# Lightning attention and a SiLU layer on one core: how the decay rates are spread, the gates of the first loads, the turn of set 5 and the form of one product are changed

## Chip, cores and metric

The kernel runs on one core of a Trainium2 chip. The metric is the device time of one execution in microseconds (us). The kernel before takes 201.95 us, the median of three runs (201.56 to 202.51).

## What is computed

The inputs are q, k, v of shape (4 batches, 8 heads, 768 positions, 64), one decay rate `lam` per head, and the weights `w_in` (512 x 2048) and `w_out` (2048 x 512), all float32.

1. Attention with decay, block by block of 64 positions (12 blocks). Inside a block, `out = ((q k^T) * Dmask) v`, with `Dmask[i,j] = lam^i` for `i >= j` and 0 elsewhere. From the blocks before, `out += (q * lam^(i+1)) state`. Then `state = lam^64 * state + (k * lam^(63-i))^T v`.
2. The heads are laid side by side: x has 3072 rows of 512 numbers.
3. `h = x w_in`, `g = h * sigmoid(h)` (SiLU), `out = g w_out`.

Nearly all arithmetic is in the two dense products of step 3.

## The kernel before

**Units, sets, groups.** A unit is 128 positions of one batch, (n, b) with n = 0..5 and b = 0..3. Units are numbered by their turn: units 0 to 7 are those of n = 0 and 1 (two of each batch in turn), units 8 to 23 are n = 2 to 5. A set is two units that are loaded together (twelve sets; sets 0 to 3 are the paired blocks n = 0, 1 of a batch, sets 4 to 11 two batches of one n). A group is the set of units whose x is multiplied by `w_in` together: groups 0 to 3 are sets 0 to 3 (256 rows), groups 4 to 7 have four units (512 rows).

**The path of a set.** SyncE's queue (SP) loads q, k, v as float32 into `raw` (512 KB each, `load_set`, L382, issued in L394 and L399). VectorE (DVE) and ScalarE (ACT) scale and cast them to bfloat16 (`kq`, `vd`). q, k are then turned (positions and features exchanged) into `kqT`: for sets below TURNED = 6 by TensorE (PE) through a bank of PSUM, matmuls `tr` of L535 (sets 0 to 3) and L722 (sets 4 and 5), and a copy by DVE or ACT; from set 6 on by a transposing DMA on SP's queue (L731). Scores (`st_ps`, L610, L766), states (`d_ps`, L557, L756) and outputs (`x_ps`, L636, L641, L788, L796) follow on PE, with masks and state sums on DVE between them. The result is copied to `xt`.

**The dense products.** Product 1 (`product1`, L917, matmuls L934, SiLU L946) takes `xt` and `w_in_bf`; half of group 6 and all of group 7 use `product1_spared` (L1052), a Strassen-like form with 7 products of blocks in place of 8. Product 2 has a plain form (`product2_plain`, L956, matmul L969: 16 matmuls of 512 columns for a unit, then one copy and one store) for the first PLAIN = 4 units, and a spared form (`product2`, L1120, matmuls L1182) for every four units after that: 7 products of 16 matmuls of 256 columns. The spared form needs 16 sums of g on DVE for each four units (L1142), and sums of `w_out` made once (`sums_of_w_out`, L1101).

**The rates.** `lam` (8 numbers) is loaded into all 128 partitions by one DMA on ACT's queue (L277). ACT takes the logarithm (L326, L328) and exponentials with a scale for each partition (L334 to L337); these multiply q, k's carry and v. ACT then loads the table for SiLU (L338). DVE first clears the six `xe` tiles (L287) and makes the scales `pose` (L321, L322).

**Weights.** POOL's queue (GpSimd) loads `w_in` in pieces i0, i1a, i1b, i2, i3 (L420) and `w_out` in o0 to o3 (L423), float32 in DRAM and bfloat16 in SBUF. A gate is a small copy (L374) on POOL, or a tiny DMA (L453) on SP, that waits for one load; what is behind it on its queue comes later. SEQUENCE (L246) gives the order: `i0@0.2` is i0 behind a gate on load 2 of set 0. Load 0 is k, 1 is q, 2 is v; for sets 0 to 3 q is issued first.

```
SEQUENCE = "s0 i0@0.2 s1 i1a@0.2 i1b i2 i3 o0 o1 s2@1.2 o2 o3 s3 s4"
```

**The order of the work** is made by a planner (class `Planner`, L38) when the program is built: each task has a key and a cost, the planner simulates engines, buffers and transfers, and emits each engine's instructions in the order of its simulated time. On the chip each engine runs its list in that order. The numbers in L35 to L47 (bytes and ns of a packet, when an engine begins, when a transfer starts and lands, until when PE is slow) are only estimates of the planner: they change the order, not the work. `filler` (L1264) puts matmuls of `ident` that nobody reads into PE's idle time at the start (between DENSE[0] and THIN).

Of the kernel before, what the change touches and what calls it, by code (L numbers as in the profile page):

```python
# [8 lines left out]
F32 = mybir.dt.float32  # L9
BF16 = mybir.dt.bfloat16  # L10
AF = mybir.ActivationFunctionType
AL = mybir.AluOpType
# [19 lines left out]

SMALL, WIDE, CAST, LARGE, HALF, TURN, PART = (256, 17.5, 20.0), (512, 25.0, 28.0), (256, 14.0, 31.0), (2048, 86.0, 86.0), (1024, 58.0, 58.0), (1024, 50.0, 50.0), (1024, 45.0, 45.0)  # L35


class Planner:  # L38
# [3 lines left out]
    OVERLAP = {"ACT": 0.1, "DVE": 0.09}  # L42
    BEGIN = {"PE": 0.8, "ACT": 7.7, "DVE": 4.5, "POOL": 4.7, "SP": 0.8}
    BIAS = {"DVE": 0.2}
    SLOW, SLOWER = 14.0, 1.8
    DENSE, THIN, REST = (9.6, 17.0), 24.0, 0.3
    FIRST, LAST, AHEAD = {"SP": 1.7, "ACT": 1.15, "POOL": 3.0}, 1.0, 0.75  # L47

    def __init__(self, pools):
        self.pools = {n: list(range(c)) for n, c in pools.items()}  # L50
# [12 lines left out]
    def order(self):  # L63
# [7 lines left out]
        free = dict(self.BEGIN)  # L71
# [56 lines left out]
        while len(out) < len(self.tasks) + fillers:  # L128
# [9 lines left out]
            for e in free:  # L138
# [2 lines left out]
                    heapq.heappush(ready[e], (key, i, t))  # L141
                if free[e] > now:
                    continue
                if e == "SP" and sum(j[2] for j in queues[e]) > self.AHEAD:
                    continue
                kept, took, short = [], None, set()
                while ready[e]:
# [53 lines left out]
                    if not u.left:  # L201
                        arm(u)
                if t.nbytes:
                    start = max(free[e] + self.FIRST[e], queues[e][-1][1] if queues[e] else 0.0)
                    queues[e].append([t, start, t.nbytes, t.kind])
                    after = transfer(now)
                else:
                    t.end = free[e] + self.LAT[e]
                    finish(t, e)
# [7 lines left out]
def kernel(  # L217
# [24 lines left out]
    PAIRED = 2  # L242
    SETS = [[(0, b), (1, b)] for b in range(B)] + [[(n, b), (n, b + 1)] for n in range(PAIRED, NB) for b in (0, 2)]
    GROUPS = SETS[:4] + [[(n, b) for b in range(B)] for n in range(PAIRED, NB)]
    FRESH, TURNED, ALONE, LEAD = 4, 6, 6, 4.5
    SEQUENCE = "s0 i0@0.2 s1 i1a@0.2 i1b i2 i3 o0 o1 s2@1.2 o2 o3 s3 s4"  # L246
    POOLS = dict(bank=8, ra=3, rb=6, kq=3, kqT=3, vd=3, st=3, xe=6, xf=3, y=2, yf=2,
                 xt2=2, xt4=2, g=18, s=12, m=3, osb=3, one=3, two=8, att=6, sp=2)
    BY_POOL, PLAIN = (), 4
    CASTING, SUMS_AFTER, HURRY, SUMS_ON, HOLD, ONTO = 12, 16, 0.0, 9.0, 1, 24  # L250
    EARLY, PACE = 1.0, 1.0
    OPEN, FILLED, SCALED = 4, True, ()
    QUERIES = (0, 1, 2, 3)
    SCORED, SOON, HALVED = (0, 1), 3, 0
    ON_ACT = ()
    LAZY, FINE, SAFE = 2.0, True, 0.3
    XE_2, XE_B, XE_P = {"ACT": 0.42, "DVE": 0.35}, 0.1, False
    MIXED, APART, KEPT = (0, 1), 1, "yf"
    EAGER, CALM, ON = 8.0, 1.0, 0.0

    ctx.enter_context(tc.manual_schedule())
    const = ctx.enter_context(tc.tile_pool(name="const", bufs=1))
# [6 lines left out]
    def tile_of(b, shape, dt, name):  # L269
# [3 lines left out]
        return b.tile  # L273


    lam_sb = const.tile([128, H], F32, name="lam_sb")
    nc.scalar.dma_start(  # L277
        out=lam_sb,
        in_=bass.AP(tensor=lam.tensor, offset=lam.offset, ap=[[0, 128]] + list(lam.ap)),
    )  # L280
    nc.scalar.preload_act_table_set("natural_log_exp_and_others")

    halves = [slice(0, 64), slice(64, 128)]
# [41 lines left out]
    log_lam = const.tile([128, NP], F32, name="log_lam")  # L325
    nc.scalar.activation(log_all, lam_sb, AF.Ln)  # L326
    for h, r in enumerate(halves):
        nc.scalar.activation(log_lam[r], lam_sb[r, h::2], AF.Ln)  # L328
    lam_v, lam_q = [const.tile([128, H], F32, name=f"lam_{x}") for x in "vq"]
    lam_v2, lam_q2 = [const.tile([128, H, 2], F32, name=f"lam_{x}2") for x in "vq"]  # L330
    lam_be = const.tile([128, NP], F32, name="lam_be")
    for i, t in ((1, lam_q2), (0, lam_v2)):
        for a in range(2):
            nc.scalar.activation(t[:, :, a], log_all, AF.Exp, scale=pose_2[:, i, a:a + 1])  # L334
    for i, t in enumerate((lam_v, lam_q)):
        nc.scalar.activation(t, log_all, AF.Exp, scale=pose[:, i:i + 1])
# [45 lines left out]
    def load_set(key, si):  # L382
        n, b = sets[si][0]
        nb = 2
        rs = [Buf("rb") if si >= CASTING and i == 0 else None if si >= CASTING and i == 1 else Buf("ra" if si in (0, 3) else "rb")
              for i in range(3)]
        ts = []
        x = [t[b, :, 0:2 * U, :].rearrange("h (p e) d -> p h (e d)", e=2) if n < PAIRED else
             t[b:b + 2, :, n * U:n * U + U, :].rearrange("b h s d -> s (b h) d") for t in (k, q, v)]

        def go(e, i):
            if n < PAIRED:
                tile_of(rs[i], [128, H, 2, 64], F32, "raw")
                nc.sync.dma_start(out=rs[i].tile.rearrange("p h e d -> p h (e d)"), in_=x[i])  # L394
            elif si >= CASTING and i < 2:
                tl = tile_of(rs[0], [128, 2, 2, NP, 2, 64], BF16, "kq")
                nc.gpsimd.dma_start(out=tl[:, i].rearrange("p b m h d -> p (b m h) d"), in_=x[i])
            else:
                nc.sync.dma_start(out=tile_of(rs[i], [128, 2 * H, 64], F32, "raw"), in_=x[i])  # L399

        for i in (1, 0, 2) if si in QUERIES else range(3):
            if si >= CASTING and i < 2:
                t = pool_task(add((key, i), {"POOL": 0.8}, lambda e, i=i: go(e, i), bufs=[rs[0]], nbytes=0.524, kind=CAST,
                                  prior=pool_last[-1:] + raw[si - 1][1][2], late=2.0))
                ts.append([t])
# [10 lines left out]
    def load_w(key, what, j, part):  # L416
        def go(e):
            if what == "i":
                cs = {"": slice(512 * j, 512 * j + 512), "a": slice(512 * j, 512 * j + 256), "b": slice(512 * j + 256, 512 * j + 512)}[part]
                nc.gpsimd.dma_start(out=w_in_bf[:, :, cs], in_=w_in_r[:, :, cs])  # L420
            else:
                ks = slice(4 * j, 4 * j + 4)
                nc.gpsimd.dma_start(out=w_out_bf[:, ks, :], in_=w_out_r[:, ks, :])  # L423

        t = pool_task(add((key, 0), {"POOL": 0.8}, go, [], [], 0.5243 if part else 1.0486,
                          PART if part else LARGE, prior=pool_last[-1:], late=1.0))
        wload.setdefault((what, j), []).append(t)
        for h in ("a", "b") if not part else part:
            wload[what, j, h] = t
# [875 lines left out]
```

## Time and profile before

| | us |
|---|---|
| median of three runs | 201.95 |
| the profiled execution | 202.37 |
| its span, from the first instruction to the last | 200.6 |
| mean granted TensorE clock | 0.997 |
| PE busy | 186.8 |
| DVE busy | 147.1 |
| ACT busy | 120.3 |
| POOL busy | 11.4 |
| first matmul of product 1 (L934) starts at | 18.70 |
| last wait of PE ends at | 54.42 |
| last matmul of PE ends at | 197.5 |

The span is that of one profiled execution, and 1.8 us of the execution lie around it. A busy PE is not PE at its peak, since matmuls overlap; where a row counts matmuls over a stretch, the stretch divided by the count is the pace. "Idle before, and what ended it" names for each group what the engine last waited for. Idle time of an engine that nobody waits for costs nothing.

### The profile page before, as it was taken

How to read it: one execution, taken by the hardware profiler on the slowest of the kernel's cores; microseconds unless marked ns; L12 is line 12 of the kernel's file. 1: busy time of each engine (PE TensorE's matmuls, PEld its weight loads, DVE VectorE, ACT ScalarE, POOL GpSimd, SP SyncE). 2: the span in 40 equal slices, each digit the busy share in tenths (PEclk: the TensorE clock that was granted, in tenths of full speed). 3: DMA queues.
4: the chain of work that ended last, by engine and by line, in shares of the span. 5: the costliest groups of instructions: out<-in, count | busy, mean ns of one | idle time of the engine just before them, and what ended most of it. 6: DMA issues, size and time to landing. Idle time of an engine off the chain costs nothing.

```text
span 200.6 us, 6005 instructions
## 1 busy us (share of the span) xinstructions
PE 186.8 (93%) x2592; PEld 142.9 (71%) x2608; DVE 147.1 (73%) x303; ACT 120.3 (60%) x225; POOL 11.4 (6%) x33
## 2 busy tenths in 40 slices
PE   0489999999899999999999999999999999999993
PEld 0468787556588785567778756478887588888882
DVE  6399620594996999989997675999969865736611
ACT  3947766374598755836363483933675878676220
POOL 6092000300000000000000000000000000000000
PEclk9999999999999999999999999999999999999998
DMA  3999999999999998999999999901811000103303
GB/s 91 299 278 202 216 218 241 275 194 232 251 261 257 220 259 144 208 220 172 273 192 241 234 251 156 216 0 57 153 61 56 3 0 13 42 2 105 107 27 131
DMA packets 85500, 32.89 MB, mean 164 GB/s; under 512 B 62946, under 2 KB 84962, under 8 KB 85474
## 3 DMA queue, kind: packets, MB, share of 16 engines
q1 hardware_dynamic: 75074, 22.55, 57.2%
q0 software_dynamic: 4752, 4.19, 13.0%
q10 hardware_dynamic: 5648, 5.77, 8.9%
q8 instruction: 20, 0.33, 0.7%
q14 instruction: 6, 0.05, 0.1%
HBM read 27.27 MB, written 6.29 MB: 167 GB/s over the span
## 4 chain that ended last, share of the span: by engine, by line
PE 70%; DMA 20%; SPq 4%; DVE 2%; issue 1%; ACT 1%; POOL 0%; DVEq 0%
PE o_ps L1182 30%; PE h_ps L934 22%; DMA raw<-in_v_dram 10%; DMA raw<-in_k_dram 10%; PE h_ps L1052 9%; SPq L394 4%; PE x_ps L796 2%; DVE wsum L353 2%; PE d_ps L756 1%; PE x_ps L788 1%; PE o_ps L969 1%; PE st_ps L766 1%; PE tr L722 1%; ACT xt L346 1%; SPq L453 0%
## 5 line engine op out<-in xcount | busy, mean ns | idle before, releaser
L934 PE MATMUL h_ps<-xt,w_in_bf 128*128 128x256 bf16 (+1 forms) x407 | 66.0, 312 | 0.7 <-DVE xt L348 0.2
L934 PEld LDWEIGHTS <-w_in_bf 128*128 128x128 bf16 x416 | 39.7, 98 | 21.1 <-DVE xt L348 0.5
L946 ACT ACTIVATE g<-h_ps 128x512 bf16<-128x512 f32 x72 | 41.9, 595 | 18.8 <-PE h_ps L934 18.4
L1182 PEld LDWEIGHTS <-g 128*128 128x128 bf16 x320 | 31.2, 98 | 4.4
L1182 PEld LDWEIGHTS <-s 128*128 128x128 bf16 x240 | 23.5, 98 | 3.4
L353 DVE TENSOR_TENSOR st<-st_ps,tri 128x512 bf16<-128x512 f32 x32 | 20.4, 682 | 2.3 <-PE st_ps L766 2.2
L353 DVE TENSOR_TENSOR osb<-o_ps,m 128x512 f32<-128x512 f32 (+1 forms) x18 | 10.7, 600 | 14.3 <-ACT m L346 8.9
L353 DVE TENSOR_TENSOR kq<-raw,lam_q 128x512 bf16<-128x512 f32 x24 | 15.9, 685 | 7.1 <-DMA raw<-in_q_dram 5.2
L346 ACT ACTIVATE m<-o_ps 128x512 f32<-128x512 f32 (+1 forms) x16 | 8.5, 529 | 20.0 <-PE o_ps L1182 20.0
L1182 PE MATMUL o_ps<-w_out_bf,s 128*128 128x256 bf16 x160 | 19.1, 273 | 0.0
L353 DVE TENSOR_TENSOR vd<-raw,lam_v 128x512 bf16<-128x512 f32 x24 | 15.9, 685 | 4.3 <-DMA raw<-in_v_dram 4.2
L1182 PE MATMUL o_ps<-wsum,g 128*128 128x256 bf16 x160 | 18.9, 273 | 0.0
L1182 PE MATMUL o_ps<-w_out_bf,g 128*128 128x256 bf16 x160 | 18.6, 273 | 0.0
L346 ACT ACTIVATE xt<-x_ps 128x512 bf16<-128x512 f32 x18 | 11.0, 644 | 10.1 <-PE x_ps L796 9.5
L969 PE MATMUL o_ps<-w_out_bf,g 128*128 128x512 bf16 x57 | 14.6, 379 | 0.6 <-issue 0.3
L353 DVE TENSOR_TENSOR h<-h_ps,m 128x512 f32<-128x512 f32 x12 | 8.3, 689 | 7.6 <-ACT m L346 6.4
L535 PE MATMUL tr<-ident,kq 128*128 128x128 bf16 x64 | 6.1, 243 | 7.9 <-DVE kq L353 7.4
L346 ACT ACTIVATE kq<-raw 128x512 bf16<-128x512 f32 x18 | 10.9, 625 | 3.5 <-DMA raw<-in_k_dram 3.5
L535 PEld LDWEIGHTS <-kq 128*128 128x128 bf16 x64 | 4.5, 108 | 9.2 <-DVE kq L353 7.6
L1052 PEld LDWEIGHTS <-wsum 128*128 128x128 bf16 x96 | 9.4, 98 | 1.3
L353 DVE TENSOR_TENSOR s<-g 128x512 bf16<-128x512 bf16 x20 | 8.2, 420 | 2.8 <-ACT g L1076 1.1
L1182 PE MATMUL o_ps<-wsum,s 128*128 128x256 bf16 x80 | 9.6, 273 | 0.0
(88 smaller groups left out, 241.7 us busy)
## 6 DMA issues: line engine op xcount, KB each, us to landing
raw<-in_q_dram SPq DMA_DIRECT2D x12, 512.0 KB, 7.6
raw<-in_k_dram SPq DMA_DIRECT2D x12, 512.0 KB, 7.6
raw<-in_v_dram SPq DMA_DIRECT2D x12, 512.0 KB, 7.9
out_dram<-osb ACTq DMA_DIRECT2D x20, 256.0 KB, 4.0
w_out_bf<-in_moe_w_out_dram POOLq DMA_DIRECT2D x4, 512.0 KB, 14.8
w_in_bf<-in_moe_w_in_dram POOLq DMA_DIRECT2D x3, 512.0 KB, 12.1
w_in_bf<-in_moe_w_in_dram POOLq DMA_DIRECT2D x2, 256.0 KB, 8.5
out_dram<-osb ACTq DMA_DIRECT2D x4, 128.0 KB, 1.7
```

Of the source, the lines that this page charges most:

```text
L346: nc.scalar.activation(o, i, AF.Copy)
L353: (nc.vector if e == "DVE" else nc.gpsimd).tensor_tensor(o, a, b, op=op)
L394: nc.sync.dma_start(out=rs[i].tile.rearrange("p h e d -> p h (e d)"), in_=x[i])
L535: nc.tensor.transpose(t[:, m, a], o.kq_of()[:, i, m, a], ident)
L722: nc.tensor.transpose(t[:, i, m, :], kq_of()[:, i, j, m], ident)
L756: nc.tensor.matmul(d_of(c)[rp, j, m, :], lhsT=o.kq_of()[r, 0, j, m, p, :], rhs=o.vd_of()[r, j, 2 * m + p, :], start=j == 0 and m == 0, sto ...
L796: nc.tensor.matmul(x_of(c)[:, j, m, :], lhsT=o.xe[c].tile[:, (bs[0] + j) % 2, m, :], rhs=o.kqT_of()[:, 1, j, m, halves[c]], start=False, s ...
L934: nc.tensor.matmul(t[:, j, :], lhsT=w_in_bf[:, ko, 128 * (m1 + j):128 * (m1 + j) + 128], rhs=xt[gi].tile[:, ko, :], start=(ko == 0), stop= ...
L946: nc.scalar.activation(t[:, half * per:half * per + per], bank.tile, AF.Silu)
L969: nc.tensor.matmul(t, lhsT=g.tile[:, j, 128 * gp:128 * gp + 128], rhs=w_out_bf[:, ko, :], start=(ko == 0), stop=(ko == KO - 1))
L1052: nc.tensor.matmul(t[:, j, :], lhsT=W[w]()[:, k2, f:f + 128], rhs=X(r)[:, k2, :], start=first and j == 0 and k2 == 0, stop=True, skip_grou ...
L1182: nc.tensor.matmul(t[:, i_, :], lhsT=src(j)[:, k2, 128 * r:128 * r + 128], rhs=W[w]()[:, 2 * j + k2, :], start=first and i_ == 0 and j == ...
```

## The change

Five things change.

1. **Rates.** `lam` is loaded into one partition (32 bytes). DVE splits it into three bfloat16 parts (four small instructions, behind the clearing of the first four `xe` tiles and ahead of the last two), and PE spreads them over the partitions with three matmuls of a row of ones. ACT takes the logarithm from PSUM; the logarithm for the carry (L328, two instructions) goes, and its exponential is made in two halves.
2. **Gates.** Both first sets are ahead of the weights in the order, and i0 waits for q of set 1 (`@1.1`) in place of v of set 0. i1a has no gate of its own. The gates of set 2 (on v of set 1) and of o2 (on k of set 2) stay.
3. **Planner's estimates.** First load sooner and faster, landings sooner (EASY, SURE, TAIL), POOL's loads start sooner, PE warm at 12.2 in place of 14.0, fillers from 7.6 in place of 9.6, more loads ahead (1.1 in place of 0.75 MB) until 16 us.
4. **Set 5** is turned by a transfer (TURNED = 5): 16 transposing matmuls (L722) and their four copies go, one transposing DMA on SP comes.
5. **Units 4 to 7** have product 2 in its plain form (PLAIN = 8): four units of 16 matmuls of 512 columns, in place of 112 matmuls of 256 columns; their 16 sums of g, three copies and four additions go, four copies and stores of a unit come. The buffer of one sum of `w_in` (S3) comes from another pool.

```diff
+FIRST_TWO = (512, 23.5, 23.5)
-SMALL, WIDE, CAST, LARGE, HALF, TURN, PART = (256, 17.5, 20.0), (512, 25.0, 28.0), (256, 14.0, 31.0), (2048, 86.0, 86.0), (1024, 58.0, 58.0), (1024, 50.0, 50.0), (1024, 45.0, 45.0)
+SMALL, WIDE, CAST, LARGE, HALF, TURN, PART = (256, 17.5, 20.0), (512, 25.0, 28.1), (256, 14.0, 31.0), (2048, 86.0, 86.0), (1024, 58.0, 58.0), (1024, 50.0, 50.0), (1024, 45.0, 45.0)
-    SLOW, SLOWER = 14.0, 1.8
-    DENSE, THIN, REST = (9.6, 17.0), 24.0, 0.3
-    FIRST, LAST, AHEAD = {"SP": 1.7, "ACT": 1.15, "POOL": 3.0}, 1.0, 0.75
+    SLOW, SLOWER = 12.2, 1.8
+    DENSE, THIN, REST = (7.6, 16.0), 23.0, 0.3
+    FIRST, LAST, AHEAD = {"SP": 1.7, "ACT": 1.15, "POOL": 2.0}, 1.0, 0.75
+    OPENING = 1.4
...
-                if e == "SP" and sum(j[2] for j in queues[e]) > self.AHEAD:
+                if e == "SP" and sum(j[2] for j in queues[e]) > (1.1 if now < 16.0 else self.AHEAD):
...
-                    start = max(free[e] + self.FIRST[e], queues[e][-1][1] if queues[e] else 0.0)
+                    start = max(free[e] + (self.OPENING if e == "SP" and now < 1.0 else self.FIRST[e]), queues[e][-1][1] if queues[e] else 0.0)
...
-    FRESH, TURNED, ALONE, LEAD = 4, 6, 6, 4.5
-    SEQUENCE = "s0 i0@0.2 s1 i1a@0.2 i1b i2 i3 o0 o1 s2@1.2 o2 o3 s3 s4"
+    FRESH, TURNED, ALONE, LEAD = 4, 5, 6, 4.5
+    SEQUENCE = "s0 s1 i0@1.1 i1a i1b i2 i3 o0 o1 s2@1.2 o2 o3 s3 s4"
-    BY_POOL, PLAIN = (), 4
+    BY_POOL, PLAIN = (), 8
-    LAZY, FINE, SAFE = 2.0, True, 0.3
+    LAZY, FINE, SAFE, EASY, TAIL, SURE = 2.0, True, 0.3, -0.22, 0.8, 1.5
+    S3_IN = "rb"
...
     nc.scalar.dma_start(
-        out=lam_sb,
-        in_=bass.AP(tensor=lam.tensor, offset=lam.offset, ap=[[0, 128]] + list(lam.ap)),
+        out=lam_sb[0:1],
+        in_=bass.AP(tensor=lam.tensor, offset=lam.offset, ap=[[0, 1]] + list(lam.ap)),
     )
...
-    for t in xe_tiles:
+    for t in xe_tiles[:4]:
+        nc.vector.memset(t, 0.0)
+    row = slice(0, 1)
+    nc.vector.tensor_copy(lam_parts[row, 0], lam_sb[row])
+    nc.vector.tensor_tensor(lam_rest[row], lam_sb[row], lam_parts[row, 0], op=AL.subtract)
+    nc.vector.tensor_copy(lam_parts[row, 1], lam_rest[row])
+    nc.vector.tensor_tensor(lam_parts[row, 2], lam_rest[row], lam_parts[row, 1], op=AL.subtract)
+    for i in range(3):
+        nc.tensor.matmul(lam_ps, lhsT=ones[row], rhs=lam_parts[row, i], start=i == 0, stop=i == 2)
+    for t in xe_tiles[4:]:
         nc.vector.memset(t, 0.0)
...
-    nc.scalar.activation(log_all, lam_sb, AF.Ln)
-    for h, r in enumerate(halves):
-        nc.scalar.activation(log_lam[r], lam_sb[r, h::2], AF.Ln)
+    nc.scalar.activation(log_all, lam_ps, AF.Ln)
...
+    for h, r in enumerate(halves):
+        nc.scalar.activation(lam_be[r], log_all[r, h::2], AF.Exp, scale=float(U))
...
-    nc.scalar.activation(lam_be, log_lam, AF.Exp, scale=float(U))
...
-                           kind=WIDE if n < PAIRED else SMALL, late=0.3 if si < 2 else SAFE if si < FRESH else 3.0)])
+                           kind=FIRST_TWO if not si and i == 1 else WIDE if n < PAIRED else SMALL, late=EASY if si < 2 else SAFE if si < FRESH else SURE)])
...
-                          PART if part else LARGE, prior=pool_last[-1:], late=1.0))
+                          PART if part else LARGE, prior=pool_last[-1:], late=TAIL - 0.3 * (what == "i" and j == 0)))
...
-        bufs = {name: Buf("kq" if name == "S3" else "rb") for name in ("S1", "S2", "S3", "S4")}
+        bufs = {name: Buf(S3_IN if name == "S3" else "rb") for name in ("S1", "S2", "S3", "S4")}
```

More of the change, by code (lines that the diff above doesn't have):

```diff
@@ L277 @@
     nc.scalar.dma_start(
-        out=lam_sb,
-        in_=bass.AP(tensor=lam.tensor, offset=lam.offset, ap=[[0, 128]] + list(lam.ap)),
+        out=lam_sb[0:1],
+        in_=bass.AP(tensor=lam.tensor, offset=lam.offset, ap=[[0, 1]] + list(lam.ap)),
     )
     nc.scalar.preload_act_table_set("natural_log_exp_and_others")
+    ones = const.tile([128, 128], BF16, name="ones")
+    nc.vector.memset(ones[0:1], 1.0)
+    lam_parts = const.tile([128, 3, H], BF16, name="lam_parts")
+    lam_rest = const.tile([128, H], F32, name="lam_rest")
     halves = [slice(0, 64), slice(64, 128)]
     xe_tiles = [const.tile([128, 2, NP, 128], BF16, name=f"xe{i}") for i in range(POOLS["xe"])]
-    for t in xe_tiles:
+    for t in xe_tiles[:4]:
[5 more added lines that the diff above has]
+    nc.vector.tensor_tensor(lam_parts[row, 2], lam_rest[row], lam_parts[row, 1], op=AL.subtract)
+    lam_ps = ps.tile([128, H], F32, tag=f"bank{POOLS['bank'] - 1}", name="lam_ps")
+    for i in range(3):
+        nc.tensor.matmul(lam_ps, lhsT=ones[row], rhs=lam_parts[row, i], start=i == 0, stop=i == 2)
+    for t in xe_tiles[4:]:
         nc.vector.memset(t, 0.0)
@@ L324 @@
     log_all = const.tile([128, H], F32, name="log_all")
-    log_lam = const.tile([128, NP], F32, name="log_lam")
-    nc.scalar.activation(log_all, lam_sb, AF.Ln)
-    for h, r in enumerate(halves):
-        nc.scalar.activation(log_lam[r], lam_sb[r, h::2], AF.Ln)
+    nc.scalar.activation(log_all, lam_ps, AF.Ln)
     lam_v, lam_q = [const.tile([128, H], F32, name=f"lam_{x}") for x in "vq"]
```

## Prediction

> **What bounds the kernel now.** I read four views. First the page: the engines and the 40 slices of 5 us.
>
> ```profile
> PE 186.8 (93%) x2592; PEld 142.9 (71%) x2608; DVE 147.1 (73%) x303; ACT 120.3 (60%) x225; POOL 11.4 (6%) x33
> PE   0489999999899999999999999999999999999993
> DVE  6399620594996999989997675999969865736611
> ```
>
> PE is full from the fourth slice to the last but one; DVE is full in stretches only, above all from 65 to 105 us. Second, the waits of PE:
>
> ```profile
> PE tr L535 <- DVE kq L353: 7.4, 2, 7.1
> PE st_ps L610 <- DVE st L353: 0.4, 1, 0.4
> ```
>
> 7.1 us of it is the start; every other wait is 0.4 us or less. By the table of 5 us windows PE is idle for 1.2 us between 20 and 55, and for 0.05 a window after that. Third, the chain of waits, start and length of each piece:
>
> ```profile
> 7.98 7.15 DMA raw<-in_v_dram
> ...
> 52.47 1.29 DVE wsum L353 x2
> 53.76 0.61 DVE st L353
> 54.38 0.04 issue
> 54.42 0.41 PE st_ps L610 x14
> ...
> 123.10 8.58 PE h_ps L934 x39
> ...
> 185.26 12.24 PE o_ps L1182 x112
> 197.50 0.02 issue
> 197.52 0.42 DVE osb L353
> ```
>
> From 54.42 to 197.5 the chain is PE alone, but for one copy of 1.1 us at 76.5 under which PE still had product 1 to do. The loads ahead of 54.42 are there only because the last gap of PE, 0.42 us, leads back to them. So the kernel is PE's work plus the start plus a tail of 3.1 us, and three things count: matmul time added or removed, the moment from which PE is full, and whether PE's stock of work lasts until the next set arrives. Fourth, the timeline of the start:
>
> ```profile
> 6.37 1.29 DVE L353 TENSOR_TENSOR kq<-raw,lam_q 128x512 bf16<-128x512 f32 x2 [1.88 <-ACT lam_q L336]
> 8.10 0.43 DVE L348 CAST kq<-raw 128x512 bf16<-128x512 f32 x1 [0.43 <-DMA raw<-in_k_dram]
> 9.98 1.29 DVE L353 TENSOR_TENSOR vd<-raw,lam_v 128x512 bf16<-128x512 f32 x2 [1.45 <-DMA raw<-in_v_dram]
> ...
> 18.70 2.79 PE L934 MATMUL h_ps<-xt,w_in_bf 128*128 128x256 bf16 x24
> ```
>
> The first row's releaser is doubtful: this task reads lam_q2 (L334), done at 5.57, not the lam_q of L336. k lands at 8.1 and v at 9.98, so loads land 1.8 to 1.9 us apart, and q on that beat lands at 6.2 to 6.3. I take it that q, not the rate, ends that wait.
>
> **Matmul time.** Plain form: the pace of 512 columns is 8.58 us for 39, 0.220; groups of four L969 stand 0.87 apart, 0.217. 64 matmuls: 13.9 to 14.1 us. Spared form: 12.24 for 112 (0.109). So +1.7 us, all on PE. Set 5's turn: four tasks of 8 transposes stand at 0.45 us each in the chain, two are set 5's: -0.9. The three matmuls of the rates lie in the 7.1 us before PE's first work. Sum **+0.8 us**.
>
> At this place the Trainium skill, page TensorE: Matmul & The Clock Gate, section Back-to-back issue gap, speaks the other way: it gives about 131 ns for each 512-column matmul in a sustained stream, and calls 216 too high. The trace does not agree (0.217 to 0.220 in streams of 39 and of 4). An estimate by that page: 64 x 0.131 = 8.4, which would make the edit -3.9 and not +1.7.
>
> **DVE, ACT, SP.** 16 sums of g go (rows of 0.42 us: 6.7 us of DVE), three copies and four additions of about 0.6 to 0.7 are replaced by four copies of 0.6, four copies of turns (0.43 to 0.6) go. I cost this at nothing: no wait of PE after 54.42 names DVE or ACT, so faster ones meet a PE that is busy. Were PE idle behind DVE there, it would be worth up to 6.7 us. The sums of w_out keep their place at 49.5; only the last (T1) moves behind units 4 to 7.
>
> Set 5's transposing DMA: the six of now take 3.0 to 6.4 us on SP's queue and land 7.1 us after issue (median), against about 2 us for transposes and copies on PE and ACT. Behind it on SP wait the loads of sets 7 and on. Those have slack: set 7 lands by about 80 and PE uses it at 99. Set 5's own use is at 71.4 (d_ps), and group 4 starts at 77.6. The cover is product 1 of groups 2 and 3, and now up to 14 us of plain product 2 that needs no sums; by 77.6 PE has done only 3.5 us of product 2 of units 4 to 7. Cost nothing; without that cover up to 5 us. The sooner landings (SURE) that the planner assumes are harmless where loads lie ready: k of set 5 lands at about 58.7 and is cast at 62.6, q is used 5 us after it lands.
>
> **The start.** One window row per us (busy of PE, PEld, DVE, ACT, POOL, then clock, DMA share, GB/s):
>
> ```profile
> 2.00:3.00 1.00, 0.00 (x0) 0.00 (x0) 0.89 (x3) 0.55 (x1) 0.89 (x5) 1.00 0.14 22
> 3.00:4.00 1.00, 0.00 (x0) 0.00 (x0) 0.89 (x3) 0.00 (x0) 0.88 (x6) 1.00 0.55 128
> 4.00:5.00 1.00, 0.00 (x0) 0.00 (x0) 0.49 (x7) 0.45 (x3) 0.48 (x3) 1.00 1.03 299
> ```
>
> Until 4 us hardly anything moves. By the packet records, 128 packets of 32 bytes (the rates) run from 2.16 to 4.49 and the first load from 2.87 to 5.56, 2.7 us where the next take 1.7 to 1.9. If one packet of rates is left, q can begin at about 2.2 (0.7 sooner) and run at 1.7 to 2.2 (0.5 to 1.0 sooner). Bounds for the loads: 0 and 1.7 us sooner; I take 1.0. The rates keep up: 32 bytes land by about 3, DVE has cleared four tiles at 3.0 (0.99 + 4 x 0.49), four small instructions of 0.07 to 0.13, three matmuls, the logarithm at 4.1; the pose scales move behind two clears to 4.5 to 4.9, so lam_q2 is ready at 5.4 (5.57 now) and q at 5.3.
>
> Product 1 starts at 18.70 behind set 1's scores and states (17.45 to 18.7), which wait for a kqT copy that ends at 18.03; xt of units 0 and 1 is ready at 17.24, and i0 lands at 17.5 by the records. Set 1's chain hangs on its loads, so it comes to 17.7. i0: its gate goes from v of set 0 (9.98) to q of set 1 (now about 11.7, then 10.7), 0.7 later; its packets start 3 us after its issue (10.65 to 13.63). But v of set 1, which shared the engines with it until 14.94, is gone by 13.9: i0 alone takes twice a half-piece's 1.56, and lands at 17.4 to 17.9. Start of the full stretch: 17.7, **1.0 us sooner**, bounds +0.3 and -1.25 (i0 as now).
>
> Does the stock last? Product 1 of groups 0 and 1 is 14 us; at 32.73, when o0 has come, 16 of its matmuls (1.75 us) are left, and at 44.85, when o2 lands, 0.4 us of the o0 and o1 work. Being 1.0 ahead eats this. The transfers after 14 us are the same bytes on engines with a share above 1 until about 48, and start only some 0.3 sooner (1.0 from the loads, less 0.7 until i0 begins). So of 1.0, about 0.7 survives at 46; and of the 1.2 us of gaps I take 0.4 off, chiefly the gap at 54, since earlier sets leave the masks room. Gain of start and stock together **1.1 us**, bounds -0.6 (below) and 2.45 (1.25 + 1.2).
>
> **Sum.** +0.8 - 1.1 = -0.3. The span goes from 200.6 to 200.3, the profiled execution from 202.37 to 202.05. That execution was 0.42 above the median of the runs, so the median becomes **201.6 us**.
>
> **Rivals.**
> - *All of the start kept.* i0 sets the start (17.45) and no gap is left: 0.8 - 2.45 = -1.65, 200.3. For it: DVE is relieved, later work is never late. Against: the thin stock at 44.85. Chance 0.18.
> - *Slower: PE runs dry of w_in.* Set 2's first load starts at 19.93, just as i1b ends, though its gate is issued at 15.15. Now the gate comes 1 us sooner. Where q of set 2 gets in beside i1a and i1b, a weight packet takes 96 ns and not 65 (records), some 1.2 us more for each half-piece. i2 lands at 25.2 and i3 at 28.8; PE, a us ahead, wants them at 26.0 and 29.5. It decides from i3 at 29.5 on: each us later is a us of idle PE. With two half-pieces displaced i3 comes at 31.2, 1.7 us of wait: 0.8 - 1.1 + 1.7 = +1.4, 203.3. Against: set 2 then lands sooner and helps at 46. Chance 0.12.
> - *It doesn't do what it says.* The slow first load is its own ramp, not the rates' packets: loads land as now, i0 is gated 1.7 us later than now (11.7) and lands at about 19.05 (3 us from issue to packets, 3.1 alone, 0.55 to land), 0.35 after 18.70. 0.8 + 0.35 = +1.15, 203.1. Chance 0.13.
> - *Set 5 comes late* and the cover fails by 3 us: 204.6. Chance 0.05.
> - *Matmuls priced by their weight loads.* If a weight load (98 ns in the rows of L969 and L1182) and not the columns set the pace, 64 cost 6.3 us against 11.0 for 112: -4.7 - 0.9 - 1.1 = -6.7, 195.2. The 39 at 0.220 speak against it. Chance 0.02. (The page named above, by its 131 ns, would stand between this and the forecast.)
>
> **How the numbers follow.** The forecast has 0.50 and by itself reaches from 200.9 to 202.5. About 0.5% (1.0 us) is what a measurement of this kernel can tell from no change; the borders are 200.95 and 202.95. Faster: 0.16 of the second case, 0.10 of the forecast, 0.02: 0.28. Slower: 0.09 + 0.08 + 0.05 + 0.01 of the forecast: 0.23. Same: 0.49. The range 200.1 to 203.5 leaves out the last two cases and the ends of the others, some 0.17.
>
> **What would show it.** Right: k and v of set 0 land at about 7 and 9 (8.1 and 9.98 now); L934 starts at 17.4 to 18.0; the L969 group has 128 matmuls near 0.22 pace and L1182 448; L722 has 16; PE busy is up by about 0.8 less fewer fillers; no wait of PE over 0.5 us after 20. Wrong: a wait of PE on w_in_bf or o0 between 25 and 46 (the dry stock), a wait for kqT of set 5 near 72, k of set 0 still at 8, or any wait of PE after 60 that names DVE, since then I have priced the relief of DVE wrongly.

## The result, and the profile after

The changed kernel takes 203.22 us (median of 22 runs), the kernel before 202.24 beside it (22 runs): the ratio is 1.0049, 95% interval 1.0027 to 1.0071. It is slower by 1.0 us, where 0.3 us faster was forecast. Three of the runs after (206.08 to 206.72) and one before (205.86) were in a slower state, as was the profiled execution of a_head below; ratios and intervals leave such runs out. The kernel after was profiled twice, in two jobs (the second is the run after_again):

| | before | after, 1st | after, 2nd |
|---|---|---|---|
| profiled execution, us | 202.37 | 203.94 | 203.14 |
| span | 200.6 | 202.2 | 201.4 |
| first product 1 starts | 18.70 | 17.45 | 17.46 |
| PE idle from there to its end | 0.81 | 2.27 | 1.83 |
| PE ends | 197.49 | 198.69 | 197.86 |
| PE's end less start less idle | 177.97 | 178.97 | 178.57 |
| from PE's end to the span's end | 3.15 | 3.55 | 3.58 |

The idle time needs care. In the first two profiles some matmul records are missing: PE x2592 for 2608 weight loads before, x2534 for 2551 after; the second profile after has 2551 of both. Where one is missing, the trace shows a gap of 0.05 us, or of 0.16 where it is the first of a group. Before has 16 such gaps and 16 missing records, after 17 and 17. Here and below they are not counted as idle.

The first execution lies 0.7 us above the median of its kernel, the second at it. So the second is the one to reckon with: start -1.25, idle +1.02, work +0.60, tail (from PE's end to the span's end) +0.43 make +0.80 of span, and 203.14 - 202.37 is +0.77.

The page of the kernel after (1st), busy time and the 40 slices of 5 us:

```profile
PE 188.5 (93%) x2534; PEld 138.1 (68%) x2551; DVE 138.2 (68%) x285; ACT 122.2 (60%) x224; POOL 10.8 (5%) x32
PE   0699999979999999999999999999999999999992
DVE  7799330497997820887899874899979645636511
```

PE is full one slice sooner (6 and not 4 in the second), and dips to 7 in the ninth, at 40 to 45 us. DVE has lost 9 us of work and is nearly empty at 70 to 80 (2 and 0), where PE is full in both kernels. PE's waits name the dip:

```profile
PE lam_ps L303 <- DVE lam_parts L297: 3.3, 1, 3.3
PE tr L551 <- DVE kq L369: 2.9, 3, 2.2
PE o_ps L985 <- DMA w_out_bf<-in_moe_w_out_dram: 1.3, 1, 1.3
```

The 7.1 us at the start are now 2.2 behind kq and 3.3 behind the rates' parts; new is a wait for weights (0.6 us in the second profile). The chain of waits (start, length, piece) runs from there to the end:

```profile
35.45 0.38 POOL gate L390
35.83 8.65 DMA w_out_bf<-in_moe_w_out_dram
44.48 0.04 issue
44.52 1.02 PE o_ps L985 x4
...
46.94 1.67 PE o_ps L985 x7
...
50.81 0.86 PE o_ps L985 x4
```

Before, the chain left the loads at 54 us with a gap of 0.42; now it leaves them at 44.5, at o2. The start itself, in the timeline of DVE and PE:

```profile
5.64 1.29 DVE L369 TENSOR_TENSOR kq<-raw,lam_q 128x512 bf16<-128x512 f32 x2 [0.31 <-ACT lam_q L349]
8.70 1.29 DVE L369 TENSOR_TENSOR vd<-raw,lam_v 128x512 bf16<-128x512 f32 x2 [0.33 <-DMA raw<-in_v_dram]
```

```profile
17.45 2.79 PE L950 MATMUL h_ps<-xt,w_in_bf 128*128 128x256 bf16 x24
```

v of set 0 is scaled 1.28 us sooner (8.70 for 9.98) and product 1 starts 1.25 sooner. The loads come sooner by the edit of the rates alone; the start of product 1 does not (b_rates, below).

### The profile page after: what moved, and what is told of

Its sections match the earlier page's. It is cut to its first block, busy times and chain, and to the rows that moved or that the text cites. A ratio compares the mean times of both kernels' runs of the same rounds, so it can differ in the third digit from the quotient of the medians.

```text
span 202.2 us, 5866 instructions
## 1 busy us (share of the span) xinstructions
PE 188.5 (93%) x2534; PEld 138.1 (68%) x2551; DVE 138.2 (68%) x285; ACT 122.2 (60%) x224; POOL 10.8 (5%) x32
## 3 DMA queue, kind: packets, MB, share of 16 engines
q0 software_dynamic: 4752, 4.19, 13.1%
## 4 chain that ended last, share of the span: by engine, by line
PE 76%; DMA 18%; SPq 3%; issue 1%; DVE 0%; POOL 0%
PE o_ps L1198 24%; PE h_ps L950 24%; PE o_ps L985 10%; DMA raw<-in_k_dram 10%; PE h_ps L1068 9%; DMA w_out_bf<-in_moe_w_out_dram 4%; DMA raw<-in_v_dram 4%; SPq L410 3%; PE x_ps L812 2%; PE d_ps L772 1%; PE x_ps L804 1%; PE st_ps L782 1%; PE x_ps L652 1%; PE tr L738 0%; PE tr L551 0%
## 5 line engine op out<-in xcount | busy, mean ns | idle before, releaser
L985 PE MATMUL o_ps<-w_out_bf,g 128*128 128x512 bf16 x119 | 28.8, 379 | 2.2 <-DMA w_out_bf<-in_moe_w_out_dram 1.3
L1198 PEld LDWEIGHTS <-g 128*128 128x128 bf16 x256 | 24.8, 98 | 3.0
L985 PEld LDWEIGHTS <-g 128*128 128x128 bf16 x128 | 12.0, 98 | 13.6 <-issue 1.6
L1198 PEld LDWEIGHTS <-s 128*128 128x128 bf16 x192 | 18.8, 98 | 2.6
L362 ACT ACTIVATE xt<-x_ps 128x512 bf16<-128x512 f32 x21 | 12.7, 642 | 11.9 <-PE x_ps L812 6.4
L369 DVE TENSOR_TENSOR osb<-o_ps,m 128x512 f32<-128x512 f32 (+1 forms) x15 | 8.7, 582 | 13.8 <-ACT m L362 6.2
L1198 PE MATMUL o_ps<-w_out_bf,s 128*128 128x256 bf16 x128 | 15.3, 272 | 0.0
L1198 PE MATMUL o_ps<-wsum,g 128*128 128x256 bf16 x128 | 15.1, 273 | 0.0
L1198 PE MATMUL o_ps<-w_out_bf,g 128*128 128x256 bf16 x128 | 15.0, 273 | 0.0
L362 ACT ACTIVATE osb<-o_ps 128x512 f32<-128x512 f32 (+1 forms) x12 | 6.7, 561 | 7.5 <-PE o_ps L985 4.8
L362 ACT ACTIVATE m<-h_ps 128x512 f32<-128x512 f32 x12 | 7.2, 597 | 4.6 <-PE h_ps L1068 4.5
```

Source lines behind the costliest of these rows:

```text
L362: nc.scalar.activation(o, i, AF.Copy)
L369: (nc.vector if e == "DVE" else nc.gpsimd).tensor_tensor(o, a, b, op=op)
L985: nc.tensor.matmul(t, lhsT=g.tile[:, j, 128 * gp:128 * gp + 128], rhs=w_out_bf[:, ko, :], start=(ko == 0), stop=(ko == KO - 1))
L1198: nc.tensor.matmul(t[:, i_, :], lhsT=src(j)[:, k2, 128 * r:128 * r + 128], rhs=W[w]()[:, 2 * j + k2, :], start=first and i_ == 0 and j == ...
```

## Experiments

"Ratio" is that to the kernel before in the same job. Runs named a_... start from the kernel after, b_... from the kernel before. The "head" is the rates, the gates and the planner's numbers; the "work" is TURNED = 5 and PLAIN = 8. Times of DMA packets below are those of the trace, from the start of the span. The packet times of the prediction and of the expectations are 0.31 us later; differences between them are not touched, but the 0.95 and 1.36 us that the expectations give from the last packet to the end are 1.26 and 1.67 here.

### Head and work apart

a_head, the head alone:

```diff
-    FRESH, TURNED, ALONE, LEAD = 4, 5, 6, 4.5
+    FRESH, TURNED, ALONE, LEAD = 4, 6, 6, 4.5
-    BY_POOL, PLAIN = (), 8
+    BY_POOL, PLAIN = (), 4
```

> The changed kernel with PLAIN = 4 and TURNED = 6, so rates, gates and estimates alone. Theory (W): the time after is the sum of three terms, the start 1.25 us sooner, 1.4 us more of PE idle (most of it the one wait of 1.34 us for o2 at 43 to 44.5), and 0.8 us more of matmul work. Then this kernel is 0.8 us under the changed one, at the time of before or 0.1 to 0.2 above it (ratio 1.000 to 1.002), product 1 starts at 17.4 to 17.6 and PE again waits about 1.3 us for w_out near 44. Rival (K): the start's gain is kept when the plan has its old amount of product 2 to place; then 1 us under before (0.995).

Measured: 202.49, ratio 1.0003 (0.998 to 1.0025). The head gains nothing, though product 1 starts a us sooner with it (17.61 in a_head_o2est, below).

b_work, the work alone, on the old head (the same two lines the other way round, in the kernel before):

> The kernel before with PLAIN = 8 and TURNED = 5 alone. W: 0.8 us of work more on a PE that is full: 0.8 us above before (1.004), PE ends at about 198.3 and starts product 1 at 18.7 as before. Rival (D): the relieved DVE or the fewer transposes give something back, so 0 to 0.3 us above before. Rival (S): set 5's transfer comes late and PE waits for it; then more than 1.2 us above before, with a wait of PE on kqT between 65 and 85.

Measured: 203.95, ratio 1.0093 (1.0076 to 1.011). PE ends at 197.40, 0.1 sooner than before: 0.24 more work, but idle time of 0.44 in place of 0.81. The 1.5 us of its span are in the **tail**, 4.7 us in place of 3.15, which no theory had. Its last copies on ACT and DVE:

```profile
196.94 0.38 ACT L346 ACTIVATE osb<-o_ps 128x256 f32<-128x256 f32 x1 [1.74 <-DMA out_dram<-osb]
```

```profile
197.96 0.76 DVE L353 TENSOR_TENSOR osb<-o_ps,m 128x256 f32<-128x256 f32 x2 [3.17 <-DMA out_dram<-osb]
```

Both wait for a buffer that a store has to leave. In the kernel before DVE's row is:

```profile
197.16 0.78 DVE L353 TENSOR_TENSOR osb<-o_ps,m 128x256 f32<-128x256 f32 x2 [2.29 <-DMA out_dram<-osb]
```

And the chain of b_work names the store (start, length), where a store of that size takes 1.7 us by the issues' median of the kernel before:

```profile
195.23 2.24 DMA out_dram<-osb
```

By the packet records, 16 KB of PE's instructions are loaded in one packet from 194.58 to 195.70; of ACT's store, 135 packets are through at 195.38 and the last 9 come between 195.70 and 196.35.

a_plain4 and a_turn6, one edit of the work each on the new head (the kernel after with PLAIN = 4, or with TURNED = 6):

> The changed kernel with PLAIN = 4 (spared form for units 4 to 7). W: 1.7 us less matmul work than the changed one, so about 0.7 us under before (0.9965), if no new wait comes. D: without the plain form DVE is full again from 65 to 105 us and PE waits for sums; then no better than the changed kernel.

> The changed kernel with TURNED = 6 (set 5 turned by PE). W: 0.9 us more of PE work: 0.9 us above the changed one, 1.9 above before (1.009). S: if set 5's transfer delays the loads behind it or group 4, taking it away gives that back, and the time is that of the changed kernel or less.

Measured: a_plain4 (TURNED = 5 alone) 205.28, ratio 1.0168 (1.0135 to 1.02); a_turn6 (PLAIN = 8 alone) 203.55, 1.0085 (1.0059 to 1.011). Over a_head, by medians and by ratios, the turn costs 2.8 to 3.3 us by itself, the plain form 1.1 to 1.7, both together 0.7 to 0.9: the edits are no sum. In a_plain4 PE waits for copies of ACT:

```profile
PE o_ps L1198 <- ACT m L362: 2.0, 2, 1.3
```

### Which part of the head gains, which loses

b_rates, the rates alone on the kernel before (DVE's and PE's part of the edit is that of the change):

```diff
...
-        out=lam_sb,
-        in_=bass.AP(tensor=lam.tensor, offset=lam.offset, ap=[[0, 128]] + list(lam.ap)),
+        out=lam_sb[0:1],
+        in_=bass.AP(tensor=lam.tensor, offset=lam.offset, ap=[[0, 1]] + list(lam.ap)),
...
-    nc.scalar.activation(log_all, lam_sb, AF.Ln)
+    nc.scalar.activation(log_all, lam_ps, AF.Ln)
```

> The kernel before with the rates spread by TensorE and nothing else: gates, planner's numbers, turn and product as before. Theory: this edit alone brings the loads of set 0 about 1.2 us sooner (v scaled at 8.7 in place of 9.98); i0, gated by v of set 0, lands 1 us sooner, product 1 starts at 17.5 to 17.9, and since the transfers of after 40 us land as before, the idle time after the start grows by as much: 1.0 within 0.003 of before. Rival K (the start is kept when the order stays that of before): 0.8 to 1.2 us below before, 0.995. Rival N (the gates or the planner's numbers brought the start, the rates nothing): first product 1 still at 18.6 to 18.8, v of set 0 still scaled at 9.9, 1.000.

Measured: 201.51, ratio 0.9965 (0.9949 to 0.9982), **the fastest of all**, faster than both kernels. The loads come sooner (v of set 0 is scaled at 8.86), but product 1 starts at 18.57, 0.13 sooner. The work is 177.81, 0.16 less, and the idle time after the start falls from 0.81 to 0.33; PE ends at 196.71, 0.8 sooner than before. The weights land sooner: i3 at 27.3 and o2 at 43.5, where before they land at 28.9 and 44.9, and after at 28.2 and 44.5 (1st) or 28.0 and 43.8 (2nd). The issue of i0 and the windows of 1 us show where the kernel after loses this lead (the last two columns are the DMA share and GB/s); first b_rates:

```profile
9.53 0.88 POOL L432 DMA_DIRECT2D w_in_bf<-in_moe_w_in_dram  x1
```

```profile
12.00:13.00 1.00, 1.00 (x32) 0.94 (x25) 1.00 (x3) 0.60 (x2) 1.00 (x3) 1.00 1.23 292
13.00:14.00 1.00, 1.00 (x24) 0.81 (x23) 1.00 (x3) 0.55 (x2) 1.00 (x2) 1.00 1.26 229
14.00:15.00 1.00, 1.00 (x38) 0.82 (x27) 1.00 (x4) 0.58 (x2) 0.98 (x2) 1.00 1.24 207
```

Then the kernel after:

```profile
11.08 3.86 POOL L436 DMA_DIRECT2D w_in_bf<-in_moe_w_in_dram  x5 [0.34 <-issue]
```

```profile
12.00:13.00 1.00, 1.00 (x38) 0.75 (x37) 1.00 (x3) 0.74 (x2) 1.00 (x2) 1.00 1.22 290
13.00:14.00 1.00, 0.95 (x23) 0.58 (x14) 1.00 (x4) 0.99 (x3) 1.00 (x2) 1.00 1.07 163
14.00:15.00 1.00, 0.83 (x16) 0.81 (x16) 1.00 (x3) 0.97 (x3) 1.00 (x3) 1.00 1.23 194
```

The GB/s of these rows must not be compared between loads and weights, since a casting load is counted by the bfloat16 that it writes. The page after shows it:

```profile
q0 software_dynamic: 4752, 4.19, 13.1%
...
HBM read 27.26 MB, written 6.29 MB: 166 GB/s over the span
```

q, k, v are 18.87 MB, so 8.39 MB of what is read is weights, twice the 4.19 MB of their queue q0. The DMA share is the measure here; where loads alone fill the engines it is 1.22 to 1.23. In both kernels the first weight packet runs at 12.9. But in b_rates i0 was issued at 9.53, and when the loads of set 1 run out the weights fill the engines at once. With i0 behind q of set 1 it is issued at 11.08, and its packets come up thinly: the share falls to 1.07 in the stretch from 13 to 14, and by the packet records 78 KB of weights move in place of 158. By 17 us the kernel after is 109 KB behind, and at 20 us still 107. This goes with the gate: in the six runs with the new rates and the old gates 141 to 162 KB of weights move from 13 to 14, in the nine with the new gates 50 to 89.

a_o2est: the planner takes o2 and o3 to land 2.0 us later, and so puts set 2's x_ps ahead of o2's products, as before; no work changes:

```diff
-                          PART if part else LARGE, prior=pool_last[-1:], late=TAIL - 0.3 * (what == "i" and j == 0)))
+                          PART if part else LARGE, prior=pool_last[-1:], late=TAIL - 0.3 * (what == "i" and j == 0) + 2.0 * (what == "o" and j > 1)))
```

> The kernel after with one number of the planner changed: it takes o2 and o3 to land 2.0 us later than it did, so that it puts the x_ps of set 2 ahead of o2's products, as the kernel before has them; no instruction is added or removed. Theory W (the order is what loses the start): PE's wait on w_out_bf at 44.5 falls from 1.33 to under 0.4, PE's idle time after the first product 1 from 2.9 to about 2.0, PE ends at about 197.8 in place of 198.69, and the time is 0.9 us below the kernel after, 1.000 of before. Rival T (the transfers themselves starve PE, whatever its order): the wait only moves to another name or a later place, the idle time stays at 2.7 to 3.0, and the time is that of the kernel after, 1.005 of before.

Measured: 203.01, ratio 1.0046 (1.0025 to 1.0067). The wait for o2 is gone from the profile and the idle time is 1.15, as the theory of the order said, but the median is only 0.1 to 0.2 below that of the kernel after and the ratios are alike: that theory falls as the main cause. The 1.33 us belonged for the most part to one execution.

a_head_o2est, the same line with PLAIN = 4 and TURNED = 6:

> The new rates, gates and planner's numbers alone (PLAIN = 4 and TURNED = 6, as in a_head), with the planner's landing of o2 and o3 2.0 us later. Theory W: PE's waits on w_out_bf after 40 us fall from 2.4 in a_head to under 1.0 and the time is 0.8 to 1.2 us below before (0.995). Rival T (starved by the transfers): idle time after the start stays near 3 us, the time is that of a_head, 1.000 of before.

Measured: 203.18, ratio 1.0054 (1.0036 to 1.0071), 1.0 us slower than a_head, against both theories. New in its profile is a wait of d_ps for vd of 0.5 at 134 us. Its idle time is 2.00 (0.33 in b_rates), and its work is 178.62, 0.8 above that of b_rates, which has the same products and turns; why is not settled.

b_work_pad, b_work with 40 matmuls that nobody reads in PE's idle start:

```diff
+    pad = ps.tile([128, 4, 128], F32, tag=f"bank{POOLS['bank'] - 1}", name="pad")
+    for i in range(40):
+        nc.tensor.matmul(pad[:, i % 4, :], lhsT=ident, rhs=ident, start=i % 4 == 0, stop=True, skip_group_check=True)
```

> The run b_work (the kernel before with PLAIN = 8 and TURNED = 5) with 40 matmuls of ident, which nobody reads, added in PE's idle start (before 7 us). They are 80 instructions of PE, so each of the 16 KB loads of PE's instructions comes some 4 us sooner in the program's work: the one at 194.9 to 196.0, which shares a DMA engine with ACT's store of 195.2, should come at about 190.5. Theory I (this load holds back the store, and so the last buffer and copy): the tail after PE's end falls from 4.7 to 3.1 to 3.5 us, and the time is 1.2 to 1.6 us below that of b_work, 1.001 to 1.004 of before. Rival P (the plain form's plan or its stores make the long tail, whatever the load does): the tail stays at 4.5 to 4.7 us, 1.008 to 1.010 of before.

Measured: 203.33, ratio 1.0062 (1.0044 to 1.0079), 0.6 us below b_work, half of what was expected. The 16 KB load is gone from the tail. Queues and issues from 194 us on, first b_work, then b_work_pad:

```profile
q8 instruction: 1, 0.02, 0.9%
...
out_dram<-osb ACTq DMA_DIRECT2D x3, 128.0 KB, 2.5
```

```profile
q14 instruction: 1, 0.01, 0.4%
...
out_dram<-osb ACTq DMA_DIRECT2D x3, 128.0 KB, 1.7
```

ACT's stores land in 1.7 us again (2.5 in b_work). From PE's end to the last packet it is 2.25 us, 2.97 in b_work, 1.89 before; PE itself ends 0.5 later, with a wait of 0.8 for w_in at 26. So the instructions' load is borne out as 0.7 us of the tail. The tail is 3.94 us, still 0.8 above that of before; 0.4 of this is settled below, under the tail.

b_rates_gates (b_rates with the new SEQUENCE; S3 goes to the pool "rb", as in the change) and b_rates_est (the kernel after with the old SEQUENCE, PLAIN = 4, TURNED = 6) part gates and planner's numbers:

```diff
-    SEQUENCE = "s0 i0@0.2 s1 i1a@0.2 i1b i2 i3 o0 o1 s2@1.2 o2 o3 s3 s4"
+    SEQUENCE = "s0 s1 i0@1.1 i1a i1b i2 i3 o0 o1 s2@1.2 o2 o3 s3 s4"
```

> The run b_rates (the kernel before with the rates spread by TensorE, 0.9965 of before) with the new order of gates, i0 behind q of set 1, and with S3 in the other pool, which the planner needs for it; planner's numbers, turn and product as before. Theory G (the gates give the start and take the weights' lead): product 1 starts at 17.4 to 17.8 in place of 18.57, but from 13 us, when set 1's loads are over, the weights move alone at 160 to 195 GB/s as in the kernel after, i3 and o2 land 0.7 to 1.1 us later than in b_rates, PE's idle time after the start is 1.0 us or more above the 0.26 of b_rates, and the time is 0.998 to 1.003 of before. Rival E (the planner's numbers are what loses it, the gates are free): the time stays at 0.993 to 0.997.

> The kernel after with the old gates, PLAIN = 4 and TURNED = 6: of the change only the rates and the planner's numbers are left. Theory G (gates): it behaves as b_rates, product 1 at about 18.5, weights 0.8 to 1.0 us sooner than before, 0.995 to 0.998 of before. Rival E (planner's numbers): the time is that of a_head and of a_head_o2est, 1.000 to 1.005.

Measured: b_rates_gates 207.86, ratio 1.0273 (1.0241 to 1.0306); b_rates_est 204.74, 1.0124 (1.0091 to 1.0156). Theory G and rival E both fail: each half alone is far worse than both halves (1.0003) or none (0.9965). The transfers do what theory G says (from 13 to 14, 72 KB of weights move in b_rates_gates and 162 in b_rates_est; i3 lands at 29.4 and 28.0), the order does not: with the new gates and the old numbers product 1 starts at 19.25, behind 12 fillers that the plan put there, although i0 had landed at 18.05; with the new numbers and the old gates it starts at 17.30, and at 24.3 PE waits for weights that the plan had sooner:

```profile
22.40 0.62 PE L1284 MATMUL ones<-ident 128*128 128x128 bf16 x8
24.32 1.05 PE L950 MATMUL h_ps<-xt,w_in_bf 128*128 128x256 bf16 x8 [1.29 <-DMA w_in_bf<-in_moe_w_in_dram]
```

b_rates_work: the work on b_rates, without gates and numbers (the two lines of a_head, the other way round).

> The run b_rates with TURNED = 5 and PLAIN = 8: the change without its gates and its planner's numbers. Theory of a sum: the two edits of work cost here what they cost on the new head (after less a_head, 0.7 us) or a little more with a long tail (1.1 us): 1.000 to 1.002 of before, PE's work up by 0.8. Rival (the weights' lead lets the plain form hide the gaps, as b_work's idle time of 0.43 shows): as b_rates, 0.997. Rival (the tail of b_work comes with it): tail of 4.5 us or more, 1.005.

Measured: 203.17, ratio 1.0051 (1.0033 to 1.007), the same as the whole change: on top of the rates the work costs 1.7 us, and then the gates and numbers cost nothing. Its PE ends at 197.06 (196.71 in b_rates; that execution, 202.63, is 0.5 below its median), its work is 0.44 more, its tail is 3.9 us (3.2).

after_again, the kernel after once more:

> The changed kernel once more, beside the others, for a second profile. If the wait of 1.33 us for o2 at 44.5 belongs to the kernel (its order), it comes again with 0.8 to 1.4 us, idle time after the start 2.4 to 3.0, and a_o2est (203.01 in the median) really is faster than it only by a wait that other runs lack or have in part. If it was an accident of the one execution, which was 0.7 us above the median of its runs, the wait is under 0.6 us, the idle time about 2.0 and the time 203.0 to 203.3.

Measured: 203.18, ratio 1.0057 (1.0034 to 1.008); the wait for o2 is 0.59, the idle time 1.83. An accident for the most part.

### The tail and the two edits of work

Of all runs, those with TURNED = 5 end 1.65 to 1.76 us after their last packet (seven profiles by then), those with TURNED = 6 1.25 to 1.28 (seven). The DMAs of SP and ACT take eight semaphores in turn; at the end SP waits for them in their order, 0.06 us each (in the kernel after from 200.94, the last landing, to 201.37). One transfer more on SP moves the last store from the eighth to the first, and seven waits come after its landing. after_lanes adds seven DMAs of four bytes ahead of SP's last four stores:

```diff
...
+            for i in range(7):
+                nc.sync.dma_start(out=spare[0:1, i:i + 1], in_=tri[0:1, i:i + 1])
```

> The kernel after with seven DMAs of four bytes on SP's queue, behind the last transposing transfer (145 us) and ahead of the last stores; nothing else moves. The DMAs of SP and ACT take eight semaphores in turn, so the last store gets the eighth again, as in the kernel before, and not the first. Theory L (at the end SP waits for the eight in their order, and TURNED = 5 had put the last landing first): the span ends 0.95 us after the last packet and not 1.36, and the time is 0.4 us below the kernel after, 1.002 to 1.004 of before. Rival (the end takes its time whatever the order, or something else than the number of transfers lengthens it): 1.36 again, 1.005.

Measured: 202.83, ratio 1.003 (1.0016 to 1.0045), 0.4 us below the kernel after: theory L holds, and the end is 1.23 us. SP's queue waits at the end of the kernel after, once, 1.3 us, for the last landing:

```profile
SPq L1316 <- DMA out_dram<-osb: 1.3, 1, 1.3
```

In after_lanes it waits twice, and the last landing is the second:

```profile
SPq L1322 <- DMA out_dram<-osb: 0.9, 2, 0.7
```

b_rates_turn5 and b_rates_turn5_lanes (b_rates with TURNED = 5, without and with the seven DMAs), and b_rates_plain8 (b_rates with PLAIN = 8, S3 in "rb"):

> The run b_rates (0.9965 of before) with TURNED = 5 alone. By the prediction's term set 5's turn takes 0.9 us off PE; by theory L the end adds 0.4: 0.994 of before, PE ends 0.9 sooner than in b_rates. Rival (DVE, which keeps the sums and copies, makes PE wait, as in a_plain4): PE ends as late as in b_rates or later, with waits of o_ps or h_ps on DVE or ACT over 0.5 us, 0.998 or more.

> The same as b_rates_turn5 with the seven DMAs of four bytes ahead of the last stores. Theory L: 0.4 us below b_rates_turn5 (0.002 of the ratio), the span ending 0.95 us after the last packet. If the prediction's term holds as well, this is the fastest of all: 0.992 of before. Rival: no difference to b_rates_turn5.

> The run b_rates (0.9965 of before) with PLAIN = 8 alone, and S3 in the other pool, which the planner needs for it. By the prediction's term the plain form adds 1.7 us of PE: 1.005 of before, PE ends 1.7 later than in b_rates, the end of the program 0.95 us behind the last packet. Rival (the sums and copies that go let PE do more of its work without short stalls): under 1.0 us, 1.001. Rival (what b_rates_work loses is the turn by transfer, not the form): as b_rates, 0.997.

Measured: b_rates_turn5 205.89, ratio 1.0177 (1.0156 to 1.0197); with the DMAs 205.79, 1.017 (1.0149 to 1.0191); b_rates_plain8 202.78, 1.0038 (1.0019 to 1.0058). The end is 1.67, 1.23 and 1.25 us. With the seven DMAs the time hardly moves there, since PE also ended 1.2 us later in that profile, behind ACT's g at 150 (1.4 us, 0.2 without); theory L is borne out by the end, not by this time.

The turn alone costs 4.3 us, where the term said -0.9. Between the profiles 3.1 of it lie before PE's end and 1.3 in the tail. PE's waits in b_rates_turn5:

```profile
PE o_ps L1194 <- DVE s L365: 1.3, 1, 1.3
PE o_ps L1194 <- ACT m L358: 1.1, 2, 0.7
```

and its windows of 5 us from 75 on, beside those of b_rates:

```profile
75.00:80.00 5.00, 4.15 (x92) 3.11 (x93) 5.00 (x13) 0.10 (x2) 0.00 (x0) 1.00 1.07 178
80.00:85.00 5.00, 3.94 (x74) 3.32 (x74) 4.55 (x10) 3.89 (x7) 0.00 (x0) 1.00 1.05 226
```

```profile
75.00:80.00 5.00, 4.93 (x71) 2.92 (x66) 4.97 (x11) 3.12 (x6) 0.00 (x0) 1.00 1.10 150
80.00:85.00 5.00, 5.00 (x35) 3.18 (x33) 5.00 (x15) 3.80 (x8) 0.00 (x0) 1.00 1.19 264
```

With the transfer, set 5's states come at 77.3 (70.6 in b_rates) and product 1 of group 4 comes after them; product 2 of units 4 to 7 is drawn forward to where DVE, full in both (5.00 and 4.97 of 5), has not made its sums. The plain form needs no sums, and turn and form together cost 1.7, not 4.3 + 1.5; that it fills this hole is argued from the two traces and not shown. The form alone costs 1.5 us (PE ends 1.3 later than in b_rates).

## Why the prediction was wrong

**The start: right, and a little small.** Loads 1.0 us sooner were forecast, 1.1 (b_rates) to 1.3 came, and product 1 at 17.45 for 17.7. This is the bound of -1.25, which the forecast put down to i0; in the trace i0 had landed at 17.33 (before at 18.25, not at 17.5 as the forecast read it), and product 1 follows the states of set 1 without a gap.

**The step that failed: "of 1.0, about 0.7 survives at 46; and of the 1.2 us of gaps I take 0.4 off", a gain of 1.1.** The idle time after the start was to fall by 0.1 net; it rose by 1.0 (2nd profile) to 1.5 (1st). Start and idle together gave 0.2 in the 2nd profile in place of 1.1, and the head by itself gave 0.0% (-0.2 to +0.25) in a_head. The 1.2 us of gaps were too much to begin with: 0.75 of them were idle time, and the rest, like the 0.05 a window, are missing records. The working had the other piece in hand, that transfers after 14 us would be only 0.3 sooner, and yet let 0.7 survive. By the bytes moved, the weights are 67 KB ahead of before at 17 us (0.35 us at the 190 KB that move in one), and 11 KB at 20. What it lacked is the price of the later gate: i0 is issued just as the loads run out, the engines are not full from 13 to 14, and the 109 KB that are missing by 17 us against b_rates are not made up. b_rates shows the other side: with the old gates i3 and o2 land 1.4 to 1.6 us sooner than before, the start stays, and 0.5 of the 0.8 us of gaps go. Start and stock are two uses of one gain, and the forecast took both.

**A term that was missing: the tail.** The forecast carried the 3.1 us over. It is 0.43 longer: 0.41 is SP's walk through the eight semaphores, which TURNED = 5 turned round (after_lanes takes it away). In b_work 0.7 us more came from a load of instructions beside the last stores; in the kernel after the 16 KB load is over in time.

**Matmul time: right in sign, rather large.** +0.8 was forecast; PE's end less start less idle rose by 0.44 (b_rates_work over b_rates), 0.24 (b_work over before) and 0.60 (after, 2nd, over before). The plain form at 0.215 (four L985 in 0.86, in the chain shown) is as reckoned. The Trainium skill, page TensorE: Matmul & The Clock Gate, section Back-to-back issue gap, which by the forecast's estimate would have made the edit -3.9 by its 131 ns, is not borne out here. But +1.7 - 0.9 is no sum of parts: alone the form costs 1.5 and the turn 4.3.

**DVE's relief and the cover of set 5: right.** No wait of PE after 60 names DVE in the kernel after, and DVE's two empty slices lie where PE was full before as well. The cover was named ("without that cover up to 5 us"), and its price is now 4.3 (b_rates_turn5) and 2.8 to 3.3 (a_plain4).

**The rivals.** None came as told, though two of them have the measured time (203.1 and 203.3): that is chance. "All of the start kept" had the right start and failed by the stock. "PE runs dry of w_in" had the right kind of wait at another place: PE ran dry of w_out, at 43 to 45, by 0.4 to 1.3 us. Its price rested on a misreading: weight packets of 96 ns are those of 1024 bytes, which take 98 ns alone too (14.8 to 15.6 in the kernel before), and the short ones, of i1a and i1b, have 512 bytes. The shift by 0.42 to the median of three runs was also too much: beside the change the kernel before had 202.24, not 201.95.

In sum, from the forecast -0.3 to the measured +0.8 between the profiles: 0.9 by start and stock, -0.2 by the work, 0.4 by the tail. What stays open: why gates or numbers alone are so dear (the orders differ on every engine), so that the gate's cost is shown for the transfers and only argued for the whole of the idle time, and where a_head_o2est lost its us.

## What to carry over

A sooner start is worth only what the transfers behind it gain as well: ask whether the bytes of the next 30 us come sooner, and read the DMA share of the stretch behind a moved gate, where the engines can run empty. Before you split a span into idle time and work, count whether matmul records are missing. Price the tail by itself, even where the change is far from it: one DMA more or less changes which semaphore ends the program, and moved instructions change where their loads fall. And two edits that free the same engine need not add: here one edit's loss, 4.3 us, was another's cover.

## What the runs showed of the hardware

- The end of the program: SP's waits for eight DMA semaphores cost 0.06 us each, so the order alone is worth 0.4 us (1.23 to 1.28 and 1.65 to 1.76 us from the last packet to the span's end).
- Instructions come by DMA while the kernel runs, on queue q8 16 KB at a time (20 packets of 0.9 to 1.6 us in the kernel after). That q8 is PE's is inferred: 80 more instructions of PE at the start bring the last of these loads 5.0 us sooner (194.58 in b_work, 189.6 in b_work_pad). In b_work a store that meets one has the last of its 16 landing signals 1.1 us behind the others (195.73 and 196.83). In b_rates_plain8, whose profiled execution is 1.0 us above its median, ACT's store has one packet of 4 bytes left at 197.22 and lands it at 197.82, behind 8 KB of instructions.
- One load of 128 packets of 32 bytes at the start held the large loads back: with one packet in its place, and nothing else of the transfers changed, v of set 0 landed 1.1 us sooner (b_rates, 8.77 for 9.88).
- The profile's GB/s counts a casting load by what it writes: 4.19 MB for 8.39 MB read.
